# A 128-column second forward pass, a GpSimd sum, and a plain fp32 inverse pass in 28 of 48 units

## The chip, the cores and the metric

The kernel runs on one NeuronCore of one Trainium2 chip. The metric is the device time of one execution in microseconds (us), as the median of three runs. Times inside the kernel come from one execution that the hardware profiler recorded.

## The reference

Three stages follow each other. Only the first one is touched by the change.

```python
X = np.fft.rfft(x, axis=1)                     # x: 4 x 3072 x 256, float32
Yr = Xr @ w_r - Xi @ w_i + b_r                 # complex mix, 256 x 256
Yi = Xr @ w_i + Xi @ w_r + b_i
Y  = soft_threshold(Yr, 0.01) + 1j * soft_threshold(Yi, 0.01)
y  = np.fft.irfft(Y, n=3072, axis=1)
...                                            # RWKV channel mix: k, v and r products
...                                            # a two-layer net with Mish
```

## The kernel before, in words

The Fourier stage fills the first 288 us. The real transform of length 3072 = 96 x 32 is done as two matrix products. The **first forward pass** (`s1`, L308) multiplies by a 96-point table and writes its result to DRAM (`scr1`). The **second forward pass** (`s2`, L357) loads it back in 48 units (4 batches of 12), tile `A`, and multiplies it by the table `MC`. A unit is then **mixed** (`mix`, L402) with the weights, put through the soft threshold, taken through the **first inverse pass** (`is1`, L448) and written to DRAM (`scr2`). The second inverse pass (L509) belongs to the next stage and begins early, in the last units.

Two kinds of fp32 product occur. A product of plain fp32 tiles is one matmul in the code and two instructions on TensorE (PE). A "split" product takes each operand as a high and a low part in the fp32r type and needs three instructions: high*high, high*low, low*high. The helper `split` makes the parts: ScalarE (ACT) casts the high part (L77), VectorE (DVE) subtracts it to get the low part (L78).

The complex mix uses three real products: `k1` from (Xr+Xi), and two more for `mxp`. Before the change the sum Xr+Xi comes out of `s2` itself, as 64 extra columns of `MC`: each unit has 192 columns instead of 128, in tile `s2p`. `split` reads `s2p` in PSUM.

One loop over u = 0 to 50 sets the order on all engines by hand; each engine works through its instructions in that order. An iteration u emits, before the change: `s2(u+1)` on PE; the eviction `Cs` of `is1(u-3)` on ACT (L460); evictions `xs` of a first pass (L316); `mix(u)` on PE with the first sum `yt<-k1p` on DVE (L405); the split of X(u+1) into `Xh`, `Xl`; background work; the second sum `yt<-mxp` (L419); the split of Y(u-1) into `Yh`, `Yl`; the threshold, which is `yc` on ACT (L423), then `Y` on DVE (L429), then three copies on GpSimd (POOL) that exchange two halves of `Y` (L431 to L433); `s1` in some units; `is1(u-2)` on PE; more background work.

`S1_AT` names the 20 units that emit a first pass for a later batch: u = 2 to 5, and from 8 to 30 two of every three. In those middle units I call the two with a first pass A and B and the third one C: A, B, C together are a **round** of the text below. The background work (`bg`) decodes 64-bit weights of the next stage on DVE (L140 to L159, L99), with a cast on ACT (L97); a round does 12 steps, which is one weight tile. From u = 33 on, `early` adds work of the next stage (`dl`, `xf`, `xk`, `xr` on DVE).

PSUM buffers before: `s2` one buffer (of two banks), `i1` one, `mx` two, `k1` one, `s1` two.

Of the kernel before, what the change touches and what calls it, by code (L numbers as in the profile page):

```python
# [29 lines left out]
def kernel(  # L30
# [27 lines left out]
    nc = tc.nc  # L58
# [13 lines left out]
    def split(src, hi, lo, lo_eng=None, hi_eng=None):  # L72

        if hi_eng is nc.vector:
            nc.vector.tensor_copy(out=hi, in_=src)
        else:
            nc.scalar.copy(out=hi, in_=src)  # L77
        (lo_eng or nc.vector).tensor_tensor(out=lo, in0=src, in1=hi, op=ALU.subtract)  # L78
# [99 lines left out]
    p1p = p1.__enter__()  # L178
# [3 lines left out]
    ps1p = ps1.__enter__()  # L182

    FC = p1sp.tile([N1, N2, N1], F32, name="FC")
    MC = p1p.tile([128, 2, 192], F32, name="MC")
    WC = p1p.tile([128, 2, 2, 128], F32R, name="WC")
    WX = p1p.tile([128, 2, 3, 2, D], F32R, name="WX")
    BIAS = p1p.tile([128, 2, 2, D], F32, name="BIAS")
# [21 lines left out]

    def split_M():
        v = cst["m"].rearrange("p (w k n) -> p w k n", w=2, k=2)[:, 0]
        sm = p1p.tile([128, 2, 64], F32, tag="K1", name="sm", bufs=1)
        re, im = v[:, :, 0:64], v[:, :, 64:128]
        nc.vector.tensor_tensor(out=sm, in0=re, in1=im, op=ALU.add)
        nc.vector.tensor_copy(out=sm[:, 1, 32:33], in_=re[:, 1, 32:33])
        nc.vector.tensor_tensor(
            out=re[:, 1, 32:33], in0=im[:, 1, 32:33], in1=re[:, 1, 32:33], op=ALU.subtract
        )
        nc.vector.memset(im[:, 1, 32:33], 0.0)  # L220
        nc.scalar.copy(out=MC[:, :, 0:128], in_=v)
        nc.vector.tensor_copy(out=MC[:, :, 128:192], in_=sm)

    def split_W():
        v = cst["m"].rearrange("p (w k n) -> p w k n", w=2, k=2)
        split(v[:, 1], WC[:, :, 0, :], WC[:, :, 1, :])

    def split_mix():
        r, i = cst["x"]
        d = [p1p.tile([128, 512], F32, tag="T", name="wd", bufs=2) for _ in range(2)]  # L230
        nc.vector.scalar_tensor_tensor(out=d[1], in0=r, scalar=-1.0, in1=i, op0=ALU.mult, op1=ALU.subtract)
        nc.vector.tensor_tensor(out=d[0], in0=i, in1=r, op=ALU.subtract)
        for c, v in ((0, r), (2, d[1]), (1, d[0])):
            v = v.rearrange("p (h n) -> p h n", h=2)
            split(v, WX[:, :, c, 0, :], WX[:, :, c, 1, :])
# [60 lines left out]
    def warm(n):  # L296
        z = p1p.tile([128, 512], F32, tag="yt", name="zero", bufs=2)
        nc.vector.memset(z[:, 0:256], 0.0)
        p = ps1p.tile([128, 2, 512], F32, tag="s2", name="warm", bufs=1)
        for _ in range(n):  # L300
            nc.tensor.matmul(out=p[:, 0, 0:256], lhsT=z[:, 0:128], rhs=z[:, 0:256], start=True, stop=True)

    def s1(b, q):
        x_ = xs_t.pop((b, q))[0:N1]
# [45 lines left out]
    def s2(u):  # L350
        last = u % NG == GS
        a = A_t.pop(u)
        p = ps1p.tile([128, 2, 512], F32, tag="s2", name="s2p", bufs=1)
        for dh in range(2):
            v = p[:, dh, 0:384].rearrange("p (c e j) -> p c e j", c=3, e=2)
            for e in range(2):
                nc.tensor.matmul(  # L357
                    out=v[:, :, e, :], lhsT=a[:, e, dh * 128:(dh + 1) * 128],
                    rhs=MC[:, int(last and e == 1), :], start=True, stop=True,
                )  # L360
        s2_t[u] = p
# [63 lines left out]

    def shrink(u):
        t, up = mx_t.pop(u)
        y = Y_t[u] = p1p.tile([128, 2, D], F32, tag="T", name="Y", bufs=2)
        nc.vector.scalar_tensor_tensor(out=y, in0=t, scalar=LAM, in1=up, op0=ALU.add, op1=ALU.min)  # L429
        w = p1p.tile([64, D], F32, tag="sw", name="sw", bufs=1)  # L430
        nc.gpsimd.tensor_copy(out=w, in_=y[64:128, 0, :])  # L431
        nc.gpsimd.tensor_copy(out=y[64:128, 0, :], in_=y[0:64, 1, :])
        nc.gpsimd.tensor_copy(out=y[0:64, 1, :], in_=w)  # L433

    def split_Y(u):
        yh = p1p.tile([128, 2, D], F32R, tag="Yh", name="Yh", bufs=2)
        yl = p1p.tile([128, 2, D], F32R, tag="Yl", name="Yl", bufs=2)
        split(Y_t.pop(u), yh, yl)
        Yh[u] = (yh, yl)

    def is1(u):
        b, g = divmod(u, NG)
        yh, yl = Yh.pop(u)
        p = ps1p.tile([128, 2, D], F32, tag="i1", name="i1p", bufs=1)
        parts = ((0, slice(0, 2)),) if g != GS else ((0, slice(0, 1)), (1, slice(1, 2)))
        for k, es in parts:
            for i, (w, v) in enumerate(((0, yh), (0, yl), (1, yh))):
                nc.tensor.matmul(  # L448
                    out=p[:, es, :], lhsT=WC[:, k, w, :], rhs=v[:, es, :], start=(i == 0), stop=(i == 2)
                )  # L450
        i1_t[u] = p
# [210 lines left out]
    later = {}  # L662
    U_E = 32
    for u in range(NU + 3):
        if 0 < u < NU - 1:
            s2(u + 1)
        if u > 2:
            is1_ev(u - 3)
        if s1_t:
            s1_ev()  # L670

        def fill():
            while s1_t:
# [36 lines left out]
        if U_E < u < NU - 1:  # L710
            early(u - U_E - 1)
# [529 lines left out]
```

## Time and profile before

| what | value |
|---|---|
| median of 3 runs | 1968.51 us (1966.07 to 1973.6) |
| the profiled execution | 1969.6 us, span of its instructions 1967.4 us |
| PE busy | 1950.6 us, 99% of the span |
| DVE busy | 1386.5 us, 70% |
| ACT busy | 1070.6 us, 54% |
| POOL busy | 94.9 us, 5% |
| PE clock granted, mean | 0.997 of full speed |

How to read it: the busy shares are means over a program of several stages. The Fourier stage is about one seventh of the span, and there all engines work at once, so what counts is who waits for whom in that stretch. A matmul row's length is longer than its slot, because matmuls are pipelined: slots are read as distances between starts.

### The profile page before, as it was taken

The page shows a single profiled execution, that of the slowest core. Times are in us where ns is not written, and L with a number is a line of the kernel's source. Part 1 is how long each engine was busy: PE and PEld are TensorE (multiplying, and loading weights), DVE is VectorE, ACT ScalarE, POOL GpSimd, SP SyncE. Part 2 cuts the span into 40 slices and gives each one's busy share as a digit, 9 for nine tenths or more (in the row PEclk, how much of TensorE's full clock was granted, in tenths as well). Part 3 has the DMA queues.
Part 4 walks back from the last instruction along what each step waited for, and adds up shares of the span by engine and source line. Part 5 has one row for each costly group of instructions (what it writes and reads, how often), then busy time and mean ns, then how long its engine had stood idle before and what let it go on. Part 6 is the DMA issues. An engine that isn't in the chain of part 4 may idle for free.

```text
span 1967.4 us, 32018 instructions
## 1 busy us (share of the span) xinstructions
PE 1950.6 (99%) x12710; PEld 1850.6 (94%) x12710; DVE 1386.5 (70%) x2135; ACT 1070.6 (54%) x1599; POOL 94.9 (5%) x188
## 2 busy tenths in 40 slices
PE   8999999999999999999999999999999999999999
PEld 5999989999999999999899999999999999999998
DVE  3899876556556555554587877777877777877785
ACT  3565657666666666666544444444444444444444
POOL 0222220000000000000000000000000000000000
PEclk9999999999999999999999999999999999999999
DMA  9777531221211211210100100100100010000000
GB/s 279 221 227 220 163 112 51 60 62 58 71 60 49 71 59 61 63 54 17 49 22 22 33 22 22 30 26 22 31 24 22 24 32 22 30 26 22 23 11 22
DMA packets 71735, 122.94 MB, mean 62 GB/s; under 512 B 6370, under 2 KB 48580, under 8 KB 71588
## 3 DMA queue, kind: packets, MB, share of 16 engines
q1 hardware_dynamic: 68004, 108.33, 18.6%
q0 software_dynamic: 3584, 12.58, 1.7%
q8 instruction: 100, 1.64, 0.4%
q14 instruction: 47, 0.39, 0.1%
HBM read 70.56 MB, written 50.33 MB: 61 GB/s over the span
## 4 chain that ended last, share of the span: by engine, by line
PE 97%; DMA 1%; DVE 1%; ACT 0%; issue 0%; SPq 0%; POOL 0%; ACTq 0%; POOLq 0%
PE h L1057 20%; PE o L1105 18%; PE kp L812 14%; PE vp L850 14%; PE o L1106 9%; PE pp L789 3%; PE p L1057 3%; PE mxp L402 3%; PE s2p L357 3%; PE pp L509 3%; PE s1p L308 2%; PE k1p L402 2%; PE i1p L448 1%; PE hp L755 1%; DMA XS<-in_x_dram 1%
## 5 line engine op out<-in xcount | busy, mean ns | idle before, releaser
L1105 PE MATMUL o<-WO,gh 128*128 128x512 f32 x1536 | 562.0, 394 | 0.0
L1106 PE MATMUL o<-WO,gl 128*128 128x256 f32 x1536 | 430.3, 280 | 0.0
L1057 PE MATMUL h<-xS,WS 128*128 128x256 f32 x2208 | 350.9, 281 | 0.0
L1105 PEld LDWEIGHTS o<-WO,gh 128*128 128x128 f32 x1536 | 288.9, 188 | 43.3
L1070 ACT COPY p1s<-p 128x256 f32<-128x256 f32 x184 | 68.8, 374 | 471.6 <-PE p L1057 470.7
L1057 PEld LDWEIGHTS h<-xS,WS 128*128 128x128 f32 x2208 | 299.6, 188 | 16.1
L837 DVE TENSOR_TENSOR kl<-kr,kh 128x768 fp32r<-128x768 f32 x128 | 122.9, 960 | 246.7 <-ACT kr L836 246.7
L812 PE MATMUL kp<-xk,WK 128*128 128x384 f32 x1536 | 295.4, 340 | 0.0
L1106 PEld LDWEIGHTS o<-WO,gl 128*128 128x128 f32 x1536 | 289.5, 188 | 0.2
L850 PE MATMUL vp<-kh,WV 128*128 128x384 f32 x1024 | 280.4, 335 | 0.0
L812 PEld LDWEIGHTS kp<-xk,WK 128*128 128x128 f32 x1536 | 268.0, 189 | 0.3
L1060 DVE TENSOR_TENSOR C<-h,p1s 128x512 f32<-128x512 f32 x184 | 127.0, 690 | 157.8 <-PE h L1057 157.8
L1042 DVE TENSOR_TENSOR gl<-g,gh 128x1024 fp32r<-128x1024 f32 x184 | 223.5, 1215 | 2.1 <-ACT g L1039 2.1
L1038 ACT ACTIVATE gh<-C 128x1024 fp32r<-128x1024 f32 x184 | 195.6, 1063 | 10.7 <-DVE C L1060 10.6
L1039 ACT ACTIVATE g<-C 128x1024 f32<-128x1024 f32 x184 | 193.0, 1049 | 0.0
L1057 PE MATMUL h<-xS,WI 128*128 128x256 f32 x1104 | 189.8, 280 | 0.0
L1060 DVE TENSOR_TENSOR C<-h,wu 128x512 f32<-128x512 f32 x368 | 187.2, 550 | 0.3 <-PE h L1057 0.3
L850 PEld LDWEIGHTS vp<-kh,WV 128*128 128x128 f32 x1024 | 186.7, 188 | 0.2 <-DVE r L858 0.2
L850 PE MATMUL vp<-kl,WV 128*128 128x384 f32 x512 | 171.5, 335 | 0.0
L835 ACT ACTIVATE kh<-kr 128x768 fp32r<-128x768 f32 x128 | 108.2, 845 | 100.5 <-PE vp L850 100.4
L1057 PEld LDWEIGHTS h<-xS,WI 128*128 128x128 f32 x1104 | 155.7, 188 | 0.0
L1060 DVE TENSOR_TENSOR wu<-h,C 128x512 f32<-128x512 f32 x184 | 126.5, 687 | 35.6 <-PE h L1057 31.8
(152 smaller groups left out, 2644.1 us busy)
## 6 DMA issues: line engine op xcount, KB each, us to landing
scr<-Cs SPq DMA_DIRECT2D x48, 256.0 KB
D<-scr SPq DMA_DIRECT2D x32, 384.0 KB
x2d<-r POOLq DMA_DIRECT2D x32, 384.0 KB, 2.8
x<-x2d SPq DMA_DIRECT2D x24, 512.0 KB
out_dram<-ob SPq DMA_DIRECT2D x96, 128.0 KB
A<-scr SPq DMA_DIRECT2D x44, 256.0 KB
xs<-in_x_dram SPq DMA_DIRECT2D x24, 384.0 KB
scr<-xs SPq DMA_DIRECT2D x24, 384.0 KB
```

The source lines that it names most:

```text
L402: nc.tensor.matmul(out=out, lhsT=a, rhs=w, start=(start and i == 0), stop=(stop and i == len(ts) - 1))
L812: nc.tensor.matmul(out=p[:, m, 0:TA], lhsT=WK[:, dh, w, f * 128:(f + 1) * 128], rhs=hl[:, v, dh, :], start=(i == 0), stop=(i == 5),)
L835: nc.scalar.activation(out=kh, in_=kr, func=AF.Square)
L837: nc.vector.tensor_tensor(out=kl, in0=kr, in1=kh, op=ALU.subtract)
L850: nc.tensor.matmul(out=p[:, o, 0:TA], lhsT=WV[:, f, w, o * 128:(o + 1) * 128], rhs=v[:, m, :], start=(f == 0 and i == 0), stop=(f == 7 and ...
L1038: nc.scalar.activation(out=gh, in_=c, func=AF.Mish)
L1039: nc.scalar.activation(out=g, in_=c, func=AF.Mish)
L1042: nc.vector.tensor_tensor(out=gl, in0=g, in1=gh, op=ALU.subtract)
L1057: nc.tensor.matmul(out=out, lhsT=a(l), rhs=xS[:, v, b, :], start=(n == 0), stop=(n == 2))
L1060: nc.vector.tensor_tensor(out=out, in0=x0, in1=x1, op=ALU.add)
L1105: nc.tensor.matmul(out=o[m], lhsT=gh[:, m2, ms], rhs=WO[:, f], start=(f == 0), stop=False)
L1106: nc.tensor.matmul(out=o[m][:, 0, :], lhsT=gl[:, m2, ms], rhs=WO[:, f, 0, :], start=False, stop=(f == 15))
```

## The change

- `MC` has 128 columns and no sum: `s2` writes 128 columns, and its PSUM tile has one bank (`i1` gets a second buffer instead).
- ACT copies `s2p` whole to SBUF, to a new tile `Xf` (L371 of the new kernel); POOL adds the two halves there to get Xr+Xi, 128 x 256 elements (L374). The split of X then reads `Xf` in SBUF instead of `s2p` in PSUM.
- `s2` and this copy run two units ahead of `mix`, the split one unit ahead as before.
- In the 28 units that are not in `S1_AT` (`whole(u)`), `is1` takes the plain fp32 `Y` and the plain table `WF` (L461): one matmul of 512 columns in two instructions instead of three split ones. `Yh` and `Yl` are not made there.

The core of the diff:

```diff
-    MC = p1p.tile([128, 2, 192], F32, name="MC")
+    MC = p1p.tile([128, 2, 128], F32, name="MC")
+    WF = p1p.tile([128, 2, 128], F32, name="WF")
...
-        p = ps1p.tile([128, 2, 512], F32, tag="s2", name="s2p", bufs=1)
+        p = ps1p.tile([128, 2, 2, 128], F32, tag="s2", name="s2p", bufs=1)
...
+    def s2_ev(u):
+        p = s2_t.pop(u)
+        v = Xf[u] = p1p.tile([128, 2, 3, 128], F32, tag="Xf", name="Xf", bufs=2)
+        nc.scalar.copy(
+            out=v[:, :, 0:2, :].rearrange("p h c j -> p h (c j)"), in_=p.rearrange("p h c j -> p h (c j)")
+        )
+        nc.gpsimd.tensor_tensor(out=v[:, :, 2, :], in0=v[:, :, 0, :], in1=v[:, :, 1, :], op=ALU.add)
+
+    def split_X(u):
...
-        split(p[:, :, 0:384], xh, xl)
-        fill()
+        split(Xf.pop(u), xh, xl)
...
     def split_Y(u):
+        if whole(u):
+            return
...
-        p = ps1p.tile([128, 2, D], F32, tag="i1", name="i1p", bufs=1)
+        p = ps1p.tile([128, 2, D], F32, tag="i1", name="i1p", bufs=2)
...
+            if whole(u):
+                nc.tensor.matmul(out=p[:, es, :], lhsT=WF[:, k, :], rhs=y[:, es, :], start=True, stop=True)
+                continue
...
-        if 0 < u < NU - 1:
-            s2(u + 1)
+        if u + 2 < NU:
+            s2(u + 2)
...
-        if 0 < u < NU - 1:
-            s2_ev(u + 1, fill)
-        else:
-            fill()
+        if u + 1 < NU:
+            split_X(u + 1)
+        fill()
+        if u + 2 < NU:
+            s2_ev(u + 2)
```

What moves on each engine, at the three places that the prediction speaks of.

**ACT, from the end of a unit B into unit C.** `L97` is the background cast of a weight, `Cs` the eviction of `is1`, `xs` those of `s1`. Before:

```order
L423 ACTIVATE yc<-yt 128x512
L97 CAST WK<-dec_v 128x512
L460 COPY Cs<-i1p 128x512
L316 COPY xs<-s1p 96x512
L77 CAST Xh<-s2p 128x768
L316 COPY xs<-s1p 96x512
L77 CAST Yh<-Y 128x512
L423 ACTIVATE yc<-yt 128x512
```

After:

```order
L428 ACTIVATE yc<-yt 128x512
L97 CAST WK<-dec_v 128x512
L476 COPY Cs<-i1p 128x512
L313 COPY xs<-s1p 96x512
L77 CAST Xh<-Xf 128x768
L313 COPY xs<-s1p 96x512
L371 COPY Xf<-s2p 128x2x256
L77 CAST Yh<-Y 128x512
L428 ACTIVATE yc<-yt 128x512
```

`Xh` keeps its place, three instructions behind `yc`. The new copy `Xf` stands behind it, ahead of `Yh`.

**DVE, one unit A** (its predecessor C is one of the 28). Before:

```order
L405 TENSOR_TENSOR yt<-k1p,BIAS 128x512
L78 TENSOR_TENSOR Xl<-s2p,Xh 128x768
L144 SCALAR_TENSOR_TENSOR dec_v<-dec_raw,dec_v 128x512
L148 TENSOR_SCALAR dec_b<-dec_v 128x512
L419 TENSOR_TENSOR yt<-mxp,yt 128x512
L78 TENSOR_TENSOR Yl<-Y,Yh 128x512
L429 SCALAR_TENSOR_TENSOR Y<-yt,yc 128x512
L150 SCALAR_TENSOR_TENSOR dec_b<-dec_raw,dec_b 128x512
```

After:

```order
L410 TENSOR_TENSOR yt<-k1p,BIAS 128x512
L78 TENSOR_TENSOR Xl<-Xf,Xh 128x768
L144 SCALAR_TENSOR_TENSOR dec_v<-dec_raw,dec_v 128x512
L148 TENSOR_SCALAR dec_b<-dec_v 128x512
L424 TENSOR_TENSOR yt<-mxp,yt 128x512
L434 SCALAR_TENSOR_TENSOR Y<-yt,yc 128x512
L150 SCALAR_TENSOR_TENSOR dec_b<-dec_raw,dec_b 128x512
```

`Xl` now has both inputs in SBUF. `Yl`, which stood between the second sum and `Y`, is gone here; in units B and C it stays.

**PE, the end of a unit with `s1` and the start of the next one.** Before:

```order
L308 MATMUL s1p<-xs,FC 96x256 x4
L448 MATMUL i1p<-Yh,WC 128x512
L448 MATMUL i1p<-Yl,WC 128x512
L448 MATMUL i1p<-Yh,WC 128x512
L357 MATMUL s2p<-MC,A 128x3x64 x4
L402 MATMUL k1p<-WX,Xh 128x256 x2
```

After, where the unit of `is1` is one of the 28:

```order
L305 MATMUL s1p<-xs,FC 96x256 x4
L461 MATMUL i1p<-Y,WF 128x512
L354 MATMUL s2p<-MC,A 128x2x64 x4
L407 MATMUL k1p<-WX,Xh 128x256 x2
L407 MATMUL k1p<-WX,Xl 128x256
```

The three split products become one plain one, and the `s2` that follows belongs to a unit one further on than before.

## Rows read from the trace of the kernel before

**Rows 1.** Windows: stretch, sum, PE, PEld, DVE, ACT, POOL busy; clock, DMA.

```profile
150.00:200.00 50.00, 50.00 (x328) 45.99 (x328) 45.90 (x74) 29.65 (x53) 14.47 (x30) 1.00 0.74 225
```

**Rows 2.** Timeline of PE, two units: start us, length us, instruction.

```profile
104.97 1.46 PE L357 MATMUL s2p<-MC,A 128*128 128x192 f32 x8
...
110.84 1.46 PE L357 MATMUL s2p<-MC,A 128*128 128x192 f32 x8
...
112.85 0.40 PE L402 MATMUL mxp<-WX,Xh 128*128 128x256 f32 x2
...
113.21 0.40 PE L402 MATMUL mxp<-WX,Xh 128*128 128x256 f32 x2
...
114.53 0.40 PE L448 MATMUL i1p<-Yl,WC 128*128 128x512 f32 x1
114.76 0.39 PE L448 MATMUL i1p<-Yh,WC 128*128 128x512 f32 x1
```

**Rows 3.** Timeline of DVE, one round; idle before and its cause in brackets.

```profile
162.51 0.96 DVE L78 TENSOR_TENSOR Xl<-s2p,Xh 128x768 fp32r<-128x768 f32 x1
...
168.90 0.68 DVE L419 TENSOR_TENSOR yt<-mxp,yt 128x512 f32<-128x512 f32 x1
...
170.33 0.69 DVE L429 SCALAR_TENSOR_TENSOR Y<-yt,yc 128x512 f32<-128x512 f32 x1 [0.16 <-ACT yc L423]
...
174.96 0.68 DVE L419 TENSOR_TENSOR yt<-mxp,yt 128x512 f32<-128x512 f32 x1
...
178.56 0.96 DVE L78 TENSOR_TENSOR Xl<-s2p,Xh 128x768 fp32r<-128x768 f32 x1 [0.22 <-ACT Xh L77]
```

**Rows 4.** Timeline of ACT, from B into C of the same round.

```profile
175.73 0.63 ACT L423 ACTIVATE yc<-yt 128x512 f32<-128x512 f32 x1 [1.85 <-DVE yt L419]
...
177.73 0.80 ACT L77 CAST Xh<-s2p 128x768 fp32r<-128x768 f32 x1
```

**Rows 5.** Timeline of DVE, unit 0, which has no Yl.

```profile
47.96 0.69 DVE L429 SCALAR_TENSOR_TENSOR Y<-yt,yc 128x512 f32<-128x512 f32 x1 [0.70 <-ACT yc L423]
```

**Rows 6.** Timelines of DVE and POOL: adds alone, and beside POOL.

```profile
73.68 0.67 DVE L154 TENSOR_TENSOR dec_v<-dec_v,dec_b 128x512 f32<-128x512 f32 x1
...
155.61 0.77 DVE L154 TENSOR_TENSOR dec_v<-dec_v,dec_b 128x512 f32<-128x512 f32 x1
...
150.73 0.40 POOL L432 COPY Y<-Y 64x256 f32<-64x256 f32 x1
...
155.11 0.73 POOL L431 COPY sw<-Y 64x256 f32<-64x256 f32 x1 [3.52 <-DVE Y L429]
...
927.11 2.41 POOL L78 TENSOR_TENSOR x2h<-x,x2h 128x1024 fp32r<-128x1024 f32 x1 [9.69 <-DVE x2h L75]
...
929.20 1.14 DVE L837 TENSOR_TENSOR kl<-kr,kh 128x768 fp32r<-128x768 f32 x1 [2.22 <-ACT kr L836]
```

**Rows 7.** Timeline of DVE, units 31 to 34, without a first pass.

```profile
211.02 0.95 DVE L78 TENSOR_TENSOR Xl<-s2p,Xh 128x768 fp32r<-128x768 f32 x1
...
218.72 0.69 DVE L405 TENSOR_TENSOR yt<-k1p,BIAS 128x512 f32<-128x512 f32 x1 [0.57 <-PE k1p L402]
...
222.87 0.69 DVE L405 TENSOR_TENSOR yt<-k1p,BIAS 128x512 f32<-128x512 f32 x1 [0.54 <-PE k1p L402]
```

**Rows 8.** Timeline of DVE, first sums of units 42 and 46.

```profile
258.92 0.69 DVE L405 TENSOR_TENSOR yt<-k1p,BIAS 128x512 f32<-128x512 f32 x1
...
277.39 0.68 DVE L405 TENSOR_TENSOR yt<-k1p,BIAS 128x512 f32<-128x512 f32 x1
```

**Rows 9.** Timelines of DVE and PE at the end of the stage.

```profile
283.12 0.69 DVE L78 TENSOR_TENSOR Yl<-Y,Yh 128x512 fp32r<-128x512 f32 x1 [0.73 <-ACT Yh L77]
...
287.04 0.79 PE L448 MATMUL i1p<-Yh,WC 128*128 128x512 f32 x1 [0.55 <-ACT Cs L460]
...
288.49 5.99 PE L812 MATMUL kp<-xk,WK 128*128 128x384 f32 x24
```

**Rows 10.** Timeline of PE at the start: the second s2.

```profile
35.10 2.00 PE L357 MATMUL s2p<-MC,A 128*128 128x192 f32 x8 [1.88 <-DVE Xl L78]
```

More of the change, by code (lines that the diff above doesn't have):

```diff
@@ L212, in split_M @@
         v = cst["m"].rearrange("p (w k n) -> p w k n", w=2, k=2)[:, 0]
-        sm = p1p.tile([128, 2, 64], F32, tag="K1", name="sm", bufs=1)
         re, im = v[:, :, 0:64], v[:, :, 64:128]
-        nc.vector.tensor_tensor(out=sm, in0=re, in1=im, op=ALU.add)
-        nc.vector.tensor_copy(out=sm[:, 1, 32:33], in_=re[:, 1, 32:33])
         nc.vector.tensor_tensor(
-            out=re[:, 1, 32:33], in0=im[:, 1, 32:33], in1=re[:, 1, 32:33], op=ALU.subtract
+            out=re[:, 1, 32:33], in0=re[:, 1, 32:33], in1=im[:, 1, 32:33], op=ALU.subtract
         )
-        nc.vector.memset(im[:, 1, 32:33], 0.0)
-        nc.scalar.copy(out=MC[:, :, 0:128], in_=v)
-        nc.vector.tensor_copy(out=MC[:, :, 128:192], in_=sm)
+        nc.scalar.copy(out=MC, in_=v)
     def split_W():
@@ L226, in split_W @@
         split(v[:, 1], WC[:, :, 0, :], WC[:, :, 1, :])
+        nc.vector.tensor_copy(out=WF, in_=v[:, 1])
     def split_mix():
         r, i = cst["x"]
-        d = [p1p.tile([128, 512], F32, tag="T", name="wd", bufs=2) for _ in range(2)]
+        d = [p1p.tile([128, 512], F32, tag="T", name="wd", bufs=3) for _ in range(2)]
         nc.vector.scalar_tensor_tensor(out=d[1], in0=r, scalar=-1.0, in1=i, op0=ALU.mult, op1=ALU.subtract)
@@ L298, in warm @@
         nc.vector.memset(z[:, 0:256], 0.0)
-        p = ps1p.tile([128, 2, 512], F32, tag="s2", name="warm", bufs=1)
+        p = ps1p.tile([128, 512], F32, tag="s2", name="warm", bufs=1)
         for _ in range(n):
-            nc.tensor.matmul(out=p[:, 0, 0:256], lhsT=z[:, 0:128], rhs=z[:, 0:256], start=True, stop=True)
+            nc.tensor.matmul(out=p[:, 0:256], lhsT=z[:, 0:128], rhs=z[:, 0:256], start=True, stop=True)
     def s1(b, q):
@@ L352, in s2 @@
         a = A_t.pop(u)
-        p = ps1p.tile([128, 2, 512], F32, tag="s2", name="s2p", bufs=1)
+        p = ps1p.tile([128, 2, 2, 128], F32, tag="s2", name="s2p", bufs=1)
         for dh in range(2):
-            v = p[:, dh, 0:384].rearrange("p (c e j) -> p c e j", c=3, e=2)
+            v = p[:, dh].rearrange("p c (e j) -> p c e j", e=2)
             for e in range(2):
@@ L361, in s2 @@
         s2_t[u] = p
+    NATIVE = True
     S1_AT = {2 + i: 4 + i for i in range(4)}
@@ L366 @@
     s2_t = {}
-    def s2_ev(u, fill=lambda: None):
-        last = u % NG == GS
-        p = s2_t.pop(u)
-        xh = p1p.tile([128, 2, 384], F32R, tag="Xh", name="Xh", bufs=2)
-        xl = p1p.tile([128, 2, 384], F32R, tag="Xl", name="Xl", bufs=2)
-        split(p[:, :, 0:384], xh, xl)
-        fill()
+    Xf = {}
+    def s2_ev(u):
[6 more added lines that the diff above has]
+    def split_X(u):
+        last = u % NG == GS
+        xh = p1p.tile([128, 2, 3, 128], F32R, tag="Xh", name="Xh", bufs=2)
+        xl = p1p.tile([128, 2, 3, 128], F32R, tag="Xl", name="Xl", bufs=2)
+        split(Xf.pop(u), xh, xl)
         Xh[u] = (xh, xl)
@@ L379, in s2_ev @@
             for k, v in enumerate((xh, xl)):
-                c = v[:, :, 96:97]
-                nc.scalar.copy(out=ZV[:, k, :, 96:97], in_=c)
+                c = v[:, :, 0:2, 96:97]
+                nc.scalar.activation(out=ZV[:, k, :, 96:97], in_=c[:, :, 0], func=AF.Copy, scale=-1.0)
                 nc.scalar.activation(out=c, in_=c, func=AF.Copy, scale=0.0)
@@ L395, in terms @@
             return [
-                (hl[a][:, dh, 128 * c:128 * c + 128], WX[:, dh, w, b, :])
+                (hl[a][:, dh, c, :], WX[:, dh, w, b, :])
                 for dh in range(2) for (a, b) in ((0, 0), (0, 1), (1, 0))
@@ L427, in shrink @@
         t, up = mx_t.pop(u)
-        y = Y_t[u] = p1p.tile([128, 2, D], F32, tag="T", name="Y", bufs=2)
+        y = Y_t[u] = p1p.tile([128, 2, D], F32, tag="T", name="Y", bufs=3)
         nc.vector.scalar_tensor_tensor(out=y, in0=t, scalar=LAM, in1=up, op0=ALU.add, op1=ALU.min)
@@ L433, in shrink, with whole @@
         nc.gpsimd.tensor_copy(out=y[0:64, 1, :], in_=w)
+    def whole(u):
+        return NATIVE and u not in S1_AT
     def split_Y(u):
+        if whole(u):
+            return
         yh = p1p.tile([128, 2, D], F32R, tag="Yh", name="Yh", bufs=2)
@@ L442, in is1 @@
         b, g = divmod(u, NG)
-        yh, yl = Yh.pop(u)
-        p = ps1p.tile([128, 2, D], F32, tag="i1", name="i1p", bufs=1)
+        if whole(u):
+            y = Y_t.pop(u)
+        else:
+            yh, yl = Yh.pop(u)
+        p = ps1p.tile([128, 2, D], F32, tag="i1", name="i1p", bufs=2)
         parts = ((0, slice(0, 2)),) if g != GS else ((0, slice(0, 1)), (1, slice(1, 2)))
         for k, es in parts:
+            if whole(u):
+                nc.tensor.matmul(out=p[:, es, :], lhsT=WF[:, k, :], rhs=y[:, es, :], start=True, stop=True)
+                continue
             for i, (w, v) in enumerate(((0, yh), (0, yl), (1, yh))):
@@ L591 @@
     s1(1, 3)
+    split_X(0)
     make_bias()
```

## The prediction

> **What bounds the kernel now.** The page puts TensorE first everywhere, so I asked at once for the windows of the Fourier stage, where all of the change lies. From 150 to 200 us TensorE is busy for all of the stretch at the full clock, but DVE is busy for 45.90 of 50 us too, and ACT for 29.65 [rows 1]. Two engines this full can both be the bound, so I read their timelines.
>
> TensorE: a unit with a first pass takes 110.84 - 104.97 = 5.87 us [rows 2], one without 222.87 - 218.72 = 4.15 us [rows 7], and no idle time stands ahead of these rows. A round A, B, C is thus 2 x 5.87 + 4.15 = 15.89 us of TensorE.
>
> DVE: from one `Xl` of a unit C to the next the round takes 178.56 - 162.51 = 16.05 us [rows 3]. Most of it is DVE work back to back. The rest are waits for ACT, not for TensorE, at two places. From the start of the second sum to the start of `Y` it is always 170.33 - 168.90 = 1.43 us [rows 3]: sum, then `yc` on ACT, then `Y`; `Yl` stands in this gap for free. And from the second sum of B to `Xl` of C it is 178.56 - 174.96 = 3.60 us [rows 3], of which 177.73 - 175.73 + 0.80 = 2.80 are `yc`, the cast `L97`, `Cs`, `xs` and `Xh` on ACT, without a pause [rows 4]. So DVE and ACT alone need 16.05 us for a round, as much as TensorE. The reader is to see two bounds of almost equal length, one behind the other.
>
> **The change part by part, TensorE.** `s2` is 8 instructions a unit. Its slot now: first-pass work is 5.87 - 4.15 = 1.72 us for 8 instructions of 256 columns, 0.215 each. A mix slot is (113.21 - 112.85) / 3 = 0.12, 18 of them 2.16; an `is1` slot is 114.76 - 114.53 = 0.23, three of them 0.69 [rows 2]. Then `s2` has 4.15 - 2.16 - 0.69 = 1.30, or 0.1625 each for 192 columns. With 128 columns it is at best 0.1625 x 128 / 192 = 0.108, at worst the 0.12 of a mix matmul, which loads as many weights. I take 0.114, the middle: 384 x 0.0485 = 18.6 us less (16.3 to 20.9).
>
> The plain `is1` is two instructions of 512 columns, each twice the plain fp32 256-column slot, 0.43: 0.86 against 0.69, so 28 x 0.17 = 4.8 us more. TensorE's work falls by 13.8 us (11.5 to 16.1). What of it reaches the end depends on DVE and ACT.
>
> **Units 8 to 31 (about 8 rounds).** `Yl` goes in C's unit of each round. In the trace a unit without `Yl` still waits for `yc`: unit 0 idles 0.70 us there [rows 5]. So this removal gives DVE nothing. `Xh` stays three instructions behind `yc`; the new copy `Xf` lies behind `xs` in time in which ACT waits (1.85 us ahead of `yc`, [rows 4]). The round stays at 16.05 us, whatever TensorE saves in it, and I count nothing won here.
>
> A cost comes in: `Xl` now reads two SBUF tensors, and POOL has a new two-input add beside it. The add of 128x1024 took 2.41 us; for 256 columns a quarter, 0.60, is my estimate. A DVE add that started while a POOL copy ran took 0.77 instead of 0.67, and one of 768 columns that started while the POOL add ran took 1.14 [rows 6] instead of 0.96 [rows 3]. With three such meetings a round at 0.10 to 0.18 each, 0.30 to 0.54, I take 0.45 a round, 3.6 us in all; the bounds are 0 (no meeting, POOL waits) and 0.6 a unit (DVE waits out a whole add).
>
> The Trainium skill, page "SBUF — State Buffer", section "Who interferes with whom", says that a DVE instruction with two SBUF inputs and a GpSimd instruction that reads SBUF exclude each other, and that the later one blocks until the first is done. The rows agree that they disturb each other but not on the size: with 929.52 as the end of the add, the DVE row should have been 0.32 longer and was 0.18. By the rule in full, with 0.60 us for each unit, the sum below would end about 13 us later; that is the third rival.
>
> Against this stands TensorE's lag. `Xl` of unit 32 ends at 211.02 + 0.95 = 211.97, and mix 32 starts at 218.72 - 0.72 - 4.15 = 213.85 (0.72 being six mix slots, [rows 2, 7]). A faster TensorE can close these 1.9 us up to the third matmul: 1.7 us won.
>
> **Units 32 to 40** wait for TensorE: DVE idles 0.54 us a unit for `k1p` [rows 7]. Here a unit falls by 8 x 0.0485 - 0.17 = 0.22 us: 2.0 us won.
>
> **Units 41 to 47** carry `dl`, `xf`, `xk`, `xr` on DVE: (277.39 - 258.92) / 4 = 4.62 us a unit without idle time [rows 8], over TensorE's 4.15. Nothing won; for meetings with POOL 1.0 us lost (0 to 2.5).
>
> **The end.** `Y` of unit 47 stands behind `Yl`, which waited 0.73 us for `Yh` [rows 9]; without it `Y` can begin when `Yl` did, at 283.12. Then 0.69 for `Y` [rows 3], three POOL copies of 0.40 with a little between them, 1.3 us (2.2 if each is disturbed as the one of 0.73 was, [rows 6]), and `is1` of 0.86: 286.0, or 286.8 at half clock, against 288.49 [rows 9]. That is 1.7 to 2.5; I take 2.2. The last three `is1` slots before took 288.49 - 287.04 = 1.45, about twice 0.69, so the clock had fallen there after an idle time; whether it still does I can't tell.
>
> **The start.** The second `s2` waited 1.88 us for `Xl` [rows 10]; now it waits for the copy alone, and the dependence of later `s2` on DVE goes. But weights and bias arrive as before, and the third `s2` now stands ahead of the first mix, behind two copies on ACT. I take 1.0 us won (0 to 3). The extra buffers, the `WF` copy on DVE and POOL's place for the sum fall into waits for DMA and count nothing; if uncovered, 0.4 us. `A` is needed one unit sooner; it is loaded five units ahead, and no row shows TensorE waiting for it.
>
> **Sum** against the profiled execution's 1969.6 us: 3.6 - 1.7 - 2.0 + 1.0 - 2.2 - 1.0 = -2.3, giving 1967.3. The shown median is 1968.51, 1.1 less; so 1966.
>
> **The rivals.**
> *TensorE sets the pace throughout* (0.24). Then nearly all of 13.8 arrives, with 3.2 from the ends: 1968.5 - 17 = 1951.5. For it: full busy time and the chain of TensorE slots. Against it: 16.05 against 15.89 us a round, and DVE waits for ACT. It would need a shorter round on DVE, which the order doesn't show.
> *The narrower pass is no cheaper* (0.10): 128 columns still take 0.1625, because weights bound them. Then units 32 to 40 cost 9 x 0.17 = 1.5 more instead of 2.0 less, and the sum rises by 3.5: about 1969.5. Against it: mix matmuls load the same weights in 0.12.
> *POOL's add blocks DVE* (0.10). It decides where DVE is the bound, at `Xl` and the decoding. Each unit of the middle loses 0.6: 1.8 a round, 14.4 us, and 3 in units 41 to 47, against 1.7 + 2.0 + 2.2 + 1.0 = 6.9 won: 1968.5 + 10.5 = 1979. It turns the sign from about 0.8 us a round (6.9 / 8).
> *My forecast* (0.56): 1959 to 1972 by itself.
>
> **Numbers.** A difference of 0.5%, 9.8 us, is about what a measurement of this kernel can tell from no change. Faster: the first rival, and a little of the forecast's low side: 0.27. Slower: most of the third: 0.08. Same: 0.65. The range 1952 to 1974 leaves out half of the first rival and most of the third.
>
> **What would show it.** Right: `s2` slots near 0.114; in the middle, rounds of 16 us or a little more with TensorE waiting for `Xl` about 1 us a round; a wait for `yc` of some 0.7 us in unit A; units 32 to 40 near 3.93 us without other work. Wrong: a round near 15 us means that DVE's chain is shorter than I read it; `Xl` rows well over 1.0 us beside POOL's add mean the third rival; an add of over 1 us would put POOL in front of `Xh`.

## The result and the profile after

The changed kernel takes 1978.96 us (median of 7 runs, 1977.53 to 1982.0) against 1968.51 us (7 runs, 1964.81 to 1973.6) beside it: ratio 1.0053, 95% interval 1.0042 to 1.0064. It is slower by about 10 us, outside the predicted range. The profiled execution took 1982.0 us, the longest of the seven, with a span of 1980.1 us; a second profile of the same kernel, taken with the experiments, has a span of 1976.7 us, and its runs a median of 1977.69 us.

The first look is at the same window of the Fourier stage as in [rows 1] (stretch, sum, PE, PEld, DVE, ACT, POOL busy; clock, DMA share, GB/s):

```profile
150.00:200.00 50.00, 45.84 (x310) 39.43 (x309) 43.82 (x65) 31.66 (x57) 22.20 (x37) 1.00 0.71 214
```

TensorE was busy for all of the 50 us; now it idles for 4.16 of them. The groups of waits of units 8 to 31 (engine, instruction, whom it waits for; us in total, times, longest) say for whom:

```profile
POOL sw L436 <- DVE Y L434: 62.4, 23, 3.9
ACT yc L428 <- DVE yt L424: 46.0, 23, 3.6
...
PE s2p L354 <- ACT Xf L371: 10.6, 7, 1.7
...
DVE Y L434 <- ACT yc L428: 8.6, 23, 0.8
DVE Xl L78 <- ACT Xh L77: 6.4, 7, 0.9
```

TensorE waits for the copy `Xf`, which frees the only PSUM buffer of `s2`; ACT and POOL wait for DVE; and DVE waits little. So DVE is late. The chain of work from 150 to 180 us, followed back from its end at each step to what released it and summed by line, was TensorE alone before; now DVE and ACT lead it and no row of TensorE is shown ("issue" is time in which the engine waited for nothing that the profile shows). Before, then after:

```profile
by line: PE mxp L402 28.8%; PE s1p L308 23.0%; PE s2p L357 22.6%; PE i1p L448 13.9%; PE k1p L402 11.9%
```

```profile
by line: issue 18.2%; DVE yt L424 12.2%; DVE Y L434 9.2%; ACT yc L428 9.0%; DVE yt L410 6.0%; DVE dec_v L154 5.2%; DVE dec_v L144 5.1%; ACT Xh L77 4.9%; DVE WV L99 4.6%; DVE dec_v L159 4.5%; DVE dec_b L150 4.1%; ACT WV L97 4.0%; ACT xs L313
```

Now the round itself, as in [rows 3]. DVE's timeline from `Xl` of one unit C to the next:

```profile
159.31 0.96 DVE L78 TENSOR_TENSOR Xl<-Xf,Xh 128x768 fp32r<-128x768 f32 x1 [0.91 <-ACT Xh L77]
...
163.78 1.00 DVE L78 TENSOR_TENSOR Xl<-Xf,Xh 128x768 fp32r<-128x768 f32 x1
164.71 1.58 DVE L144 SCALAR_TENSOR_TENSOR dec_v<-dec_raw,dec_v 128x512 int32<-128x512 int32 x1
...
166.67 0.68 DVE L424 TENSOR_TENSOR yt<-mxp,yt 128x512 f32<-128x512 f32 x1
168.10 0.69 DVE L434 SCALAR_TENSOR_TENSOR Y<-yt,yc 128x512 f32<-128x512 f32 x1 [0.76 <-ACT yc L428]
...
171.26 1.24 DVE L78 TENSOR_TENSOR Xl<-Xf,Xh 128x768 fp32r<-128x768 f32 x1
...
176.67 0.96 DVE L78 TENSOR_TENSOR Xl<-Xf,Xh 128x768 fp32r<-128x768 f32 x1 [0.91 <-ACT Xh L77]
```

and POOL's in the same two units A and B:

```profile
164.04 1.01 POOL L438 COPY Y<-sw 64x256 f32<-64x256 f32 x1
165.01 0.73 POOL L374 TENSOR_TENSOR Xf<-Xf 128x256 f32<-128x256 f32 x1
...
170.97 0.72 POOL L374 TENSOR_TENSOR Xf<-Xf 128x256 f32<-128x256 f32 x1
```

This round takes 176.67 - 159.31 = 17.36 us, 1.31 more than 16.05 [rows 3]. The reader is to see two rows: `L144` takes 1.58 us, and `Xl` of B 1.24 us, both beside POOL's add; without it they take 0.68 (before) and 0.96 (unit C). `Y` of A waits 0.76 us for `yc` where `Yl` stood, which is what the missing `Yl` leaves. The groups of DVE over units 8 to 31 give the mean (count; busy us, mean ns). Before and after:

```profile
L78 DVE TENSOR_TENSOR Xl<-s2p,Xh 128x768 fp32r<-128x768 f32 x25 | 23.7, 948 | 1.2 <-ACT Xh L77 1.1
...
L144 DVE SCALAR_TENSOR_TENSOR dec_v<-dec_raw,dec_v 128x512 int32<-128x512 int32 x7 | 4.8, 680 | 0.0
```

```profile
L78 DVE TENSOR_TENSOR Xl<-Xf,Xh 128x768 fp32r<-128x768 f32 x23 | 24.7, 1075 | 6.4 <-ACT Xh L77 6.4
...
L144 DVE SCALAR_TENSOR_TENSOR dec_v<-dec_raw,dec_v 128x512 int32<-128x512 int32 x8 | 11.2, 1404 | 0.0
```

One `L144` and three `Xl` a round make 0.72 + 3 x 0.127 = 1.10 us; the mean round of units 11 to 29 went from 16.11 to 17.24, 1.13 more. So these two groups are as large as the whole loss. What else changed in DVE's mean round cancels: `Yl` of C is gone (0.67 us less), but the wait for `yc` is 0.62 longer; the wait of `Xl` for `Xh` is 0.73 longer, but the wait for TensorE's `k1p` is gone, 0.68 a round before. Over units 8 to 31 it was, before:

```profile
DVE yt L405 <- PE k1p L402: 7.2, 10, 1.3
```

The time by stretches, each from DVE's first sum of one unit to that of another (the last two from TensorE's first `kp`, the next stage):

| stretch | before | after, first profile | after, second profile |
|---|---|---|---|
| start to unit 0 | 45.79 | 49.21 | 46.61 |
| units 0 to 8 | 40.00 | 45.28 | 44.56 |
| units 8 to 31 | 124.63 | 132.20 | 132.15 |
| units 31 to 40 | 39.12 | 37.36 | 37.36 |
| units 40 to 47 | 31.38 | 33.55 | 33.51 |
| unit 47 to `kp` | 7.58 | 5.01 | 5.00 |
| `kp` to the end | 1678.87 | 1677.50 | 1677.47 |

Units 8 to 31 lose 7.5, units 40 to 47 2.1, and units 0 to 8, of which I had expected nothing, 4.6 to 5.3. Most of the latter lies in one place. ACT, from unit 5 to unit 6:

```profile
74.85 0.21 ACT L386 ACTIVATE ZV<-Xh 128x2 fp32r<-128x2 f32 x1
77.36 0.21 ACT L387 ACTIVATE Xh<-Xh 128x4 fp32r<-128x4 f32 x1 [2.30 <-DVE Xl L78]
...
77.81 0.56 ACT L313 COPY xs<-s1p 96x512 f32<-96x512 f32 x1
```

TensorE at the same place:

```profile
74.14 1.10 PE L305 MATMUL s1p<-xs,FC 96*96 96x256 f32 x4 [0.47 <-ACT xs L313]
78.42 2.02 PE L305 MATMUL s1p<-xs,FC 96*96 96x256 f32 x4 [3.18 <-ACT xs L313]
```

Unit 6 is one of the four that hold a Nyquist column, where ACT sets a column of `Xh` to zero (L387) once `Xl` has read it. In the code before, `fill()`, which emits the second eviction `xs`, stood inside `s2_ev` between the split and this zeroing. The change puts `fill()` behind `split_X`, and so behind the zeroing. The zeroing waits for `Xl` on DVE, `xs` waits behind it, and `s1` waits for `xs`. The four `s1` behind the idle time take 2.02 us where the four ahead took 1.10: in the window from 75 to 90 us the granted clock is 0.77.

The end of the stage, to be set beside [rows 9]:

```profile
302.03 1.13 PE L461 MATMUL i1p<-Y,WF 128*128 128x512 f32 x2
302.61 4.74 PE L830 MATMUL kp<-xk,WK 128*128 128x384 f32 x24
```

The first 24 `kp` now take 4.74 us instead of 5.99: the granted clock is 1.00 from 302.6 to 307.4 us, where before it was 0.50 from 288.5 to 292, and `kp` to the end is 1.4 us shorter.

### The profile page after: what moved, and what is told of

It is laid out like the page before. It is cut to its first block, busy times and chain, and to the rows that moved or that the text cites. A ratio compares the mean times of both kernels' runs of the same rounds, so it can differ in the third digit from the quotient of the medians.

```text
span 1980.1 us, 31920 instructions
## 1 busy us (share of the span) xinstructions
PE 1946.5 (98%) x12680; PEld 1829.3 (92%) x12680; DVE 1383.5 (70%) x2104; ACT 1077.3 (54%) x1619; POOL 146.5 (7%) x236
## 4 chain that ended last, share of the span: by engine, by line
PE 89%; DVE 5%; ACT 2%; issue 2%; DMA 1%; SPq 0%; ACTq 0%; DVEq 0%
PE h L1075 20%; PE o L1123 18%; PE kp L830 14%; PE vp L868 13%; PE o L1124 9%; PE pp L807 3%; PE p L1075 3%; PE pp L525 3%; PE s1p L305 1%; PE mxp L407 1%; DVE yt L424 1%; PE hp L773 1%; PE s2p L354 1%; ACT yc L428 1%; DVE Y L434 1%
```

## The experiments

Twelve runs followed, each with the kernel before beside it on the same chip; its medians there lie between 1967.99 and 1968.51 us. "The add" is POOL's L374. Stretches are those of the table.

**The second eviction ahead of the zeroing.**

```diff
-    def split_X(u):
+    def split_X(u, fill=lambda: None):
...
         split(Xf.pop(u), xh, xl)
+        fill()
...
-            split_X(u + 1)
-        fill()
+            split_X(u + 1, fill)
+        else:
+            fill()
```

> Edit: in the changed kernel the second eviction xs of a first pass stands again between the split of X and the zeroing of its Nyquist column (as in the kernel before), not behind the zeroing. Theory: in the unit ahead of unit 6 this eviction waited on ACT behind the zeroing, which waited for a late Xl on DVE, so that TensorE idled 3.18 + 0.47 us and its clock fell; without that the stretch from the first sum of unit 0 to that of unit 8 shrinks from 45.28 us to 41 to 42, and the total from 1979 to 1975 to 1976. Rival (the stretch is long because of the slow DVE work and the late weight load alone, the eviction is only where the wait shows): the stretch stays within 1 us of 45.3 and the total at 1979.

Measured: 1973.65 us, ratio 1.0027 (1.0017 to 1.0037). Units 0 to 8 take 41.81 us, and the step from unit 5 to unit 6 5.14 us (8.68 and 7.75 in the two profiles of the changed kernel, 5.11 before). TensorE at this place:

```profile
70.23 2.32 PE L305 MATMUL s1p<-xs,FC 96*96 96x256 f32 x8 [0.35 <-ACT xs L313]
```

The wait of 3.18 us is gone, and the clock stays at 1.00 in the 15 us from 70. DVE still waits here for the late weights (2.90 us for `dec_raw`), so they are not the cause by themselves. The theory holds, with a total somewhat under the range given; in medians the place cost 4 to 5.3 us (against 1977.69 and 1978.96). The middle did not move (132.15).

**POOL only writes.**

```diff
-        nc.gpsimd.tensor_tensor(out=v[:, :, 2, :], in0=v[:, :, 0, :], in1=v[:, :, 1, :], op=ALU.add)
+        nc.gpsimd.memset(v[:, :, 2, :], 0.0)
```

> Edit: GpSimd's add Xr+Xi of each unit is replaced by a fill with zeros of the same 128x256 elements, in the same place; the sum is left out of the computation. GpSimd then writes these elements and reads nothing. Theory (the add's two SBUF inputs hold up DVE's two-input work): the rows L144 and Xl beside GpSimd come back to 0.68 and 0.96 us, a round of units 8 to 31 falls from 17.36 us to 16.0 to 16.4, the total by 8 to 11 us to 1968 to 1971. Rival A (the round is longer because DVE or ACT work from SBUF, or the additional copy Xf on ACT, costs it): the round stays at 17.2 or more and the total at 1977 or more. Rival B (the three exchange copies of GpSimd hold up as much as the add): the round falls by half, to about 16.7, and the total to 1973 to 1975.

Measured: 1968.24 us, ratio 0.9998 (0.9989 to 1.0008); round 16.35, units 8 to 31 125.50, units 40 to 47 31.88 instead of 33.5. DVE in one unit A, and POOL beside it:

```profile
170.56 1.01 DVE L78 TENSOR_TENSOR Xl<-Xf,Xh 128x768 fp32r<-128x768 f32 x1
171.49 0.88 DVE L144 SCALAR_TENSOR_TENSOR dec_v<-dec_raw,dec_v 128x512 int32<-128x512 int32 x1
```

```profile
170.82 1.00 POOL L438 COPY Y<-sw 64x256 f32<-64x256 f32 x1
171.77 0.30 POOL L374 MEMSET Xf<- 128x256 f32 x1
```

The same split reads the same SBUF tile, ACT makes the same copies, and the round is back within 0.24 of before. So rival A is out: the add is the loss. The fill is shorter than the add as well (0.30 against 0.72 us), so that the round alone doesn't tell reads from length; the rows do. `L144` falls to 0.88, not 0.68; the rest is the exchange copy L438 ahead of it: `L144` ends 0.55 behind the copy's end, although POOL's fill runs in between. A fill, which only writes, did not hold it up. Rival B holds for a small part.

**The third s2 behind the first mix.**

```diff
-        if u + 2 < NU:
+        if 0 < u and u + 2 < NU:
             s2(u + 2)
...
             mix(u)
+        if u == 0:
+            s2(2)
```

> Edit: in iteration 0 alone, the second forward pass of unit 2 is emitted behind the mix of unit 0, not ahead of it. Theory: ahead of the mix it waits on TensorE for ACT's copy Xf of unit 1, which stands behind the two bias evictions; behind it, the mix can begin when the bias products have run: the first sum of unit 0 comes at 46 to 47 us instead of 49.2, and the total falls by 2 to 3 us to 1976 to 1977. Rival (the late bias and weights set the start whatever the order): the first sum of unit 0 stays at 48.5 or later, the total within 1 us of 1979.

Measured: 1976.98 us, ratio 1.0043 (1.0026 to 1.0059). The median fits the theory, the trace doesn't: the first sum of unit 0 comes at 45.06 us, no sooner than in three variants with the old order (43.51 to 44.72), because DVE has only then finished `WC` and `WF`, which wait for ACT. Against the second run of the changed kernel (1977.69) the gain is 0.7 us, not to be told from nothing.

**No plain inverse pass.** `NATIVE = False` in place of `True`.

> Edit: no unit uses the plain fp32 first inverse pass; all 48 use the three split products, with Yh and Yl made in all units (the other parts of the change stay). Theory (the middle is bound by DVE held up by GpSimd, and the end gains by the missing Yl): the round in units 8 to 31 stays at 17.3 to 17.7 us, units 31 to 40 stay within 0.5 of 37.35, the end from unit 47 to kp goes from 5.0 to about 7 us, the total is 1979 to 1982. Rival (the plain fp32 products, 28 x 0.17 = 4.8 us, are what made the kernel slower): the total falls to 1974 to 1975.

Measured: 1984.26 us, ratio 1.0075 (1.006 to 1.009). The round is 17.24, units 31 to 40 take 37.41, unit 47 to `kp` 7.40. The rival is out: the plain pass did not make the kernel slower; without it, it is slower by 5 to 7 us, more than the 0 to 3 that I gave. Of the 4.8 us that its stretches lose against the second profile of the changed kernel, start apart, 2.4 are the end and 1.0 lies behind it.

**The kernel before with the plain pass alone** (the parts `WF`, `whole`, `split_Y` and `is1` of the change; three buffers of `Y`).

> Edit: the kernel before, with only the plain fp32 first inverse pass in the 28 units (no Yh and Yl there); s2 keeps 192 columns, GpSimd gets no add. Theory (the harm of the change is GpSimd's add beside DVE and the order of the start; the plain pass only lengthens TensorE's slot by 0.17 us and shortens the end): the round of units 8 to 31 stays at 16.1 to 16.3 us, units 31 to 40, which wait for TensorE, take 40.3 to 41 us (39.12 before, + 9 x 0.17), the end from unit 47 to kp falls from 7.58 to about 5 us, the total is 1967 to 1969. Rival (removing Yl does give DVE its 0.69 us in each round): the round falls to 15.5 and the total to 1962 to 1964.

Measured: 1966.66 us, ratio 0.9991 (0.9982 to 1.0001). Round 16.21, units 31 to 40 40.25, unit 47 to `kp` 5.13. The rival is out: the missing `Yl` shortens no round. The total is a little under the range given; `kp` to the end, which I had left out, is also 1.4 us shorter. This part of the change is harmless, perhaps worth 2 us.

**The kernel before with an idle add on POOL.**

```diff
         split(p[:, :, 0:384], xh, xl)
+        nc.gpsimd.tensor_tensor(
+            out=DS, in0=xh[:, :, 0:128].bitcast(F32), in1=xh[:, :, 128:256].bitcast(F32), op=ALU.add
+        )
         fill()
```

> Edit: the kernel before, with one added GpSimd add of 128x256 elements in each unit: it adds the two halves of Xh (SBUF) into a tile that nobody reads, and starts when Xh is written, as Xl does on DVE. Nothing waits for its result but the buffers. Theory (two SBUF reads on GpSimd hold up two-input work on DVE): Xl beside it grows from 0.95 to 1.1 to 1.7 us though one of its inputs is in PSUM, the round goes from 16.1 to 16.8 to 17.8 us, and the total rises by 6 to 14 us to 1974 to 1982. Rival A (only DVE work with both inputs in SBUF is held up, and Xl reads PSUM here): Xl stays within 0.05 of 0.95 us, the round within 0.3 of 16.1, the total within 3 us of 1968. Rival B (in the changed kernel the add was a link in the chain from s2 to mix, and its place beside DVE was no matter): nothing moves at all.

Measured: 1972.11 us, ratio 1.0019 (1.001 to 1.0028); round 16.40. DVE in one unit A, and POOL beside it:

```profile
166.87 0.95 DVE L78 TENSOR_TENSOR Xl<-s2p,Xh 128x768 fp32r<-128x768 f32 x1
167.73 1.03 DVE L144 SCALAR_TENSOR_TENSOR dec_v<-dec_raw,dec_v 128x512 int32<-128x512 int32 x1
```

```profile
167.12 0.39 POOL L437 COPY Y<-sw 64x256 f32<-64x256 f32 x1
167.49 0.72 POOL L376 TENSOR_TENSOR DS<-Xh 128x256 f32<-128x256 f32 x1
```

My theory failed in its first part, and rival A is right there: `Xl`, which reads `s2p` in PSUM, stays at 0.94 to 0.96 in all 25 units, whatever POOL does, and POOL's instructions beside it aren't slowed (0.39 and 0.72). The total rose by 3.6 us, between rival A and the theory. `L144`, with both inputs in SBUF, waits: the add ends at 168.21, `L144` at 168.76. Rival B is out, since nobody waits for this add's result. So two things together make the loss: POOL reads SBUF, and DVE reads two tensors there. `L144` did so before; the change brought the add, and an `Xl` with both inputs in SBUF. That `L144` loses 0.35 here and 0.90 in the changed kernel fits the rows: there `Xl` also holds up the copy L438 (1.01 us against 0.39), the add starts later, and `L144` meets the whole of it.

**A background step in the gap.** The eviction edit above, and:

```diff
-                bg(2 if u in S1_AT else 1)
+                bg((2 if u in S1_AT else 1) - int(whole(u - 1)))
...
             above(u)
+            if u > 2 and whole(u - 1):
+                bg(1)
             shrink(u)
```

> Edit: the changed kernel with the second eviction xs ahead of the zeroing again, and in the units that follow one of the 28 plain ones (unit A of a round, and all from 32 on) one background step is emitted between yc and Y, where Yl stood, instead of ahead of the second sum. Theory (removing Yl gave DVE nothing because it waits there 0.76 us for yc; work put in the gap makes it worth something): the wait for yc in A goes, the round falls from 17.23 to 16.7 to 16.9, the total from 1973.7 to 1969 to 1971. Rival (ACT or GpSimd sets the round and DVE only waits elsewhere): the round stays within 0.1 of 17.23 and the total within 1 us of 1973.7.

Measured: 1968.14 us, ratio 1.0000 (0.9991 to 1.0009); round 16.77. `L148` now stands in A's gap and the wait for `yc` there is 0.42 instead of 0.76. The theory holds, though the wait shrinks and doesn't go, and the total is a little under the range given: what `Yl` left free is worth something when DVE work is moved into it.

**All 48 units plain, a step in each gap.** As above with `whole` true for every unit.

> Edit: as the run with a step in the gap, and the first inverse pass is plain fp32 in all 48 units: Yl and Yh are made nowhere, and each unit from 3 on has one background step between yc and Y. Theory: DVE loses 2 x 0.69 us a round and fills two or three gaps, TensorE gains 2 x 0.17 us a round of work, for which it has 1 us of idle time: the round falls to 15.8 to 16.5 us, the total to 1962 to 1968. Rival (the gap swallows what Yl took, since a step is not always a DVE instruction): the round stays at 16.7 or more, the total at 1969 or more.

Measured: 1963.99 us, ratio 0.9977 (0.9968 to 0.9986); round 16.17. The theory holds, and this is the first variant ahead of the kernel before. `L144` still takes 1.57 beside the add.

**The changed kernel again.**

> No edit: the changed kernel once more, for a second profile of its start. In the first one the first sum of unit 0 came at 49.21 us, in three variants with the same code up to there at 43.51 to 44.72. Theory (the late start belongs to that one execution, not to the change): the first sum of unit 0 comes at 44 to 47 us here, the stretch from unit 0 to unit 8 takes 43.5 to 45.3, the median stays at 1977 to 1980. Rival (the start of the changed kernel is late as a rule): the first sum of unit 0 comes at 48.5 or later again.

Measured: 1977.69 us, ratio 1.0050 (1.0037 to 1.0064), first sum of unit 0 at 46.61. Over the eight profiles with the same order up to that sum it lies between 43.51 and 49.21, in four with the start of before between 43.64 and 45.79. The late start of the first profile belongs for the larger part to that execution. It goes with the clock: in the five of the eight in which the clock granted from 40 to 50 us is 1.00 the sum comes at 43.51 to 46.28, in the three with 0.52 to 0.66, both profiles of the changed kernel among them, at 46.61 to 49.21. Which of the two brings the other is not shown.

**The steps off the add.** As in the run with all 48 units plain (the eviction edit included), and the steps of a round placed by a table (ahead of the second sum, in the gap, at the unit's end), from which the three calls of `bg` take their counts:

```diff
+    def steps(u):
+        if u < 3:
+            return 0, 0, 0
+        if 8 <= u < 32:
+            return ((0, 2, 2), (0, 2, 3), (1, 1, 1))[(u - 8) % 3]
+        return (1, 1, 3) if u in S1_AT else (0, 1, 1)
```

> Edit: as the run with all 48 units plain, and in units 8 to 31 the background steps are placed anew: none on DVE ahead of the second sum, so that GpSimd's add stands beside the second sum (one input in PSUM); L144 and L148 (unit A), L157 and L159 (B), L99 (C) stand in the gap between yc and Y; the cast L97 moves on ACT from behind yc of B to behind Xh of C. Theory (GpSimd and DVE shut each other out when DVE reads two SBUF tensors, and not when one of them is in PSUM): L144 falls from 1.57 to 0.7 to 1.1 us, the wait of C's Xl for Xh from 0.91 to about 0.4, DVE's chain to about 14 us a round, so that TensorE sets the pace with 15.2 to 15.5 us a round in place of 16.17, and the total falls from 1964 to 1956 to 1959. Rival (the add costs the same wherever it stands, or ACT sets the round): the round stays at 15.9 or more and the total at 1961 or more.

Measured: 1958.18 us, ratio 0.9952 (0.9940 to 0.9965); round 15.28, units 8 to 31 118.66. DVE in units C and A:

```profile
156.82 0.69 DVE L418 TENSOR_TENSOR yt<-k1p,BIAS 128x512 f32<-128x512 f32 x1 [1.81 <-PE k1p L415]
157.43 0.95 DVE L78 TENSOR_TENSOR Xl<-Xf,Xh 128x768 fp32r<-128x768 f32 x1
...
162.24 0.68 DVE L432 TENSOR_TENSOR yt<-mxp,yt 128x512 f32<-128x512 f32 x1
162.84 0.97 DVE L144 SCALAR_TENSOR_TENSOR dec_v<-dec_raw,dec_v 128x512 int32<-128x512 int32 x1
164.19 0.69 DVE L442 SCALAR_TENSOR_TENSOR Y<-yt,yc 128x512 f32<-128x512 f32 x1
```

The add of this unit runs from 162.54 to 163.26; the second sum, with one input in PSUM, passes it in 0.68, and `L144` waits for it in a gap that is free anyway. `Y` no longer waits, `Xl` of C no longer waits for `Xh`, and DVE waits 1.81 us for TensorE. The chain from 150 to 180 us, by line:

```profile
by line: PE mxp L415 28.7%; PE s1p L305 23.0%; PE i1p L469 17.2%; PE s2p L354 17.1%; PE k1p L415 14.2%
```

TensorE alone. This version beats both kernels, by 10 us and 20 us.

**The same with the third s2 behind the first mix** (its edit as above).

> Edit: as the run with the steps off the add, and in iteration 0 the second forward pass of unit 2 stands behind the mix of unit 0. Theory (the start waits for data; the order of s2 there is worth little): the total is within 1.5 us of the run beside it. Rival (s2 ahead of the mix holds up the start by the wait for ACT's copy): 2 to 3 us less than the run beside it.

Measured: 1957.58 us, ratio 0.9943 (0.9930 to 0.9957), 0.6 less than beside it: no difference that shows.

**The kernel before, all plain, with these steps.**

> Edit: the kernel before with the plain fp32 first inverse pass in all 48 units and the background steps placed as in the run with the steps off the add; s2 keeps 192 columns and GpSimd has no add. Theory (without GpSimd's add the steps give DVE time that TensorE cannot use: with s2 of 192 columns a round of TensorE is 15.89 + 3 x 0.17 = 16.4 us): the round is 16.3 to 16.5 us, the total 1967 to 1970. So the narrow s2 is what the 15.28 us need. Rival (the placing of the steps alone is the gain of that run, and s2's width is no matter): the round falls below 15.8 us and the total to 1962 or less.

Measured: 1969.76 us, ratio 1.0012 (1.0003 to 1.0022); round 16.50, TensorE alone in its chain. The rival is out: the narrow `s2` is what the 15.28 us need. The change had removed work from TensorE as it was meant to; DVE could not follow.

## Why the prediction was wrong

The sum by terms, with what the stretches give (second profile; the first differs at the start):

| term | predicted | measured |
|---|---|---|
| start to the first sum of unit 0 | -1.0 | +0.8 (first profile +3.4) |
| units 0 to 8 | 0 | +4.6 |
| units 8 to 31: contention and TensorE's lag | +3.6 - 1.7 | +7.5 |
| units 32 to 40 | -2.0 | -1.8 |
| units 41 to 47 | +1.0 | +2.1 |
| the end, to `kp` | -2.2 | -2.6 |
| behind it | 0 | -1.4 |
| sum | -2.3 | +9.2 |

**The contention term was mis-sized**, 0.45 us a round against 1.1. With 8 x 1.13 = 9.0 us in place of 3.6, the sum for units 8 to 40 becomes 9.0 - 1.7 - 2.0 = 5.3; measured are 7.5 - 1.8 = 5.7. So the two gains were about right, and the size of the loss was not. I had the mechanism on the table and misread the row that prices it. From [rows 6] I concluded that a DVE instruction beside POOL's add is only disturbed, since with a full exclusion `kl` should have been 0.32 us longer and was 0.18. But a held-up instruction ends 0.13 to 0.15 us sooner behind the release than its own length, as if its first part were done while it waits. Then the row says full exclusion: the add ended at 929.52, `kl` at 930.34, 0.82 later, which is 0.96 less 0.14. The same arithmetic fits every row of after that I worked out: `Xl` of B ends at 172.50, 0.81 behind the add (171.69), and `L144` at 166.29, 0.55 (its 0.68 less 0.13) behind the add (165.74). And a DVE instruction that already waits for one POOL instruction can be passed by the next. Units 44 to 47, DVE, then POOL:

```profile
289.38 1.70 DVE L78 TENSOR_TENSOR Xl<-Xf,Xh 128x768 fp32r<-128x768 f32 x1
```

```profile
289.17 0.40 POOL L438 COPY Y<-sw 64x256 f32<-64x256 f32 x1
289.54 0.72 POOL L374 TENSOR_TENSOR Xf<-Xf 128x256 f32<-128x256 f32 x1
```

`Xl` was issued 0.16 us before the add and yet ends 0.82 us behind the add's end: it waited out the copy and then the whole add. That is how 0.68 becomes 1.58. I had also looked for the meetings at `Xl` alone; two thirds of the loss is `L144`, an instruction that the change does not touch. The 0.60 us that I took for the add was 0.72 to 0.73.

The Trainium skill, page "SBUF — State Buffer", section "Who interferes with whom", states this rule: DVE with two SBUF inputs and GpSimd's reads shut each other out, GpSimd's pure writes and DVE's single SBUF input outside its two-port modes (faster modes of some DVE operations) do not. The runs agree in all three points: `L144` 1.58 beside the add, `Xl` from PSUM 0.94 to 0.96 beside it, and `L144` 0.88, waiting for the copy and not for the fill, when POOL only writes. I had set this rule aside on the strength of one misread row.

**Units 0 to 8 were not in the sum at all.** The diff shows `fill()` behind `split_X`, and I passed over it. In four units (6, 18, 30, 42) the split is followed by the zeroing, which waits for DVE; only ahead of unit 6 is an `xs` left that is queued behind it. Undoing this gave back 4 to 5.3 us. Of the stretch, 1.8 us remain over before. Of these 1.1 lie in the step from unit 7 to unit 8 (5.64 against 4.53), where the weight step `L99` takes 1.58 us instead of 0.68 and ends 0.56 behind the end of POOL's add; when POOL only writes, the step is 4.94. The rest is not traced.

**The start** was taken as a gain of 1.0 and is none: at a granted clock of 1.00 the first sum comes at 43.51 to 46.28 us, as in the four profiles with the start of before (43.64 to 45.79). Whether the order of `s2` and mix costs something there can't be settled: the first sum varies more from run to run than by the edit.

**One reading of the kernel before was too strong**: that DVE's waits in a round are for ACT and not for TensorE. Half of them were for `k1p`. In the round of [rows 3] such a wait of 0.57 us is covered by the wait for `Xh` that ends after it; one round earlier nothing covers it:

```profile
161.77 0.69 DVE L405 TENSOR_TENSOR yt<-k1p,BIAS 128x512 f32<-128x512 f32 x1 [0.73 <-PE k1p L402]
```

That DVE and ACT alone need some 16 us holds all the same: with TensorE lighter and POOL only writing, the round was 16.35, of which 0.20 is `L144`. The predicted sign that TensorE would wait for `Xl` didn't come; it waits at `s2` for the copy `Xf`, 10.6 us in units 8 to 31.

**Right**: the missing `Yl` gives DVE nothing in the middle (the predicted wait for `yc` of some 0.7 us in A is there, 0.76); the plain pass takes 0.86 us (119.91 to 120.77 in the trace); units 32 to 40; the end, whose open point, the clock behind it, went the good way; and the slot of `s2`. A unit of TensorE without a first pass now takes 237.06 - 233.15 = 3.91 us; less 2.16 for the mix and 0.86 for `is1` that leaves 0.89, or 0.111 for each of the eight instructions, against 0.114.

**The rivals.** The third, POOL's add blocking DVE, named the mechanism and the time (1979), but its price was too high in the middle (1.8 a round against 1.1), and units 0 to 8, which it did not have, filled the sum: that the time agrees is luck. The first, TensorE's pace, fell because DVE and ACT hold the round above it, even without the add (16.35 us when POOL only writes); the run with the steps off the add shows the pace, 15.28 us, once DVE is relieved. That the narrower pass is no cheaper is out (0.111 against 0.1625).

## What to carry to other kernels

Before moving work to GpSimd that reads SBUF, list which DVE instructions near it read two SBUF tensors: here each that met the add waited to its end, and moving an input from PSUM to SBUF adds one to the list. A saving on an engine that waits (here `Yl` ahead of `yc`) is worth nothing until other work is moved into the hole. When a diff moves a call past a function, read what that function emits in its rare branches, and what then queues behind it.

## What the runs showed of the hardware that was not expected

Back-to-back GpSimd instructions keep a waiting DVE instruction out: `Xl` of 0.96 us took 1.70 beside a copy of 0.40 that had 0.19 left and an add of 0.72. It works the other way too: the copy L438, 0.40 alone, took 1.01 beside `Xl` of A. A waiting DVE instruction ends 0.13 to 0.15 us sooner behind GpSimd's end than its own length. One input is not always safe: with a step in the gap, `L148`, which reads one SBUF tensor and takes 0.43 us elsewhere, took 0.88 beside an add that began 0.13 us ahead of it (at 139.01 and 205.85 us). In two profiles of the same kernel the first sum of the stage came 2.6 us apart, at a granted clock of 0.52 and 0.53 from 40 to 50 us in both; in the kernel before it was 1.00 there. The start is no place to read a difference of 1 or 2 us.
